# A recurrent-memory transformer layer on one core: the forward output projection in 256-column halves, a float32 memory selection, and row sums on GpSimd

## The chip, the cores and the metric

The kernel runs on one core of a Trainium2 chip. Times are device microseconds of one execution of the whole program. The kernel before was run three times; the median is compared. Profiled executions are read from the hardware profiler's trace: its span runs from the first to the last instruction.

Engine names: PE is TensorE (matmuls; PEld are its weight loads), DVE is VectorE, ACT is ScalarE, POOL is GpSimd, SP is SyncE, which issues most DMAs.

## The reference

One layer and its backward pass are computed: a residual, a recurrent attention branch with memory, and a dense branch with a squared ReLU, then all gradients.

```python
# x (1,2048,512); mem0 (1,8,512); 32 heads of 128; segments of 32 tokens
xn = layernorm(x)
mem = mem0
for s in range(64):
    h = concat([mem, xn[:, 32*s:32*s+32]])        # 8 + 32 rows
    q, k, v = h @ Wq, h @ Wk, h @ Wv              # per head
    p = softmax(mask(q @ k.T * scale))
    o = einsum('bhte,hed->btd', p @ v, Wo)        # sum over 32 heads
    mem = o[:, :8]                                # memory of the next segment
    outs.append(o[:, 8:])
out = x + concat(outs) + mlp(xn)
# then the gradients of x, mem0, Wq, Wk, Wv, Wo and of the dense branch
```

The memory makes the 64 segments a sequential chain: the projections of segment s+1 need rows 0 to 7 of the output projection of segment s.

## The kernel before

**Stages.** The program has five: the dense branch and the layer norm (0 to some 230 us of the span), the forward recurrence (to some 1310 us), a stretch in which weights are turned for the backward pass (to some 1345 us), the backward recurrence (to some 2515 us), and the weight gradients (to the end). Partial results pass between the stages through DRAM tensors whose names begin with S_. Every instruction is unrolled.

**Order.** In the forward and backward stages every operation is given to a planner (`_Plan`, `plan.add`) with a cost for each engine that may run it, the keys that it reads and writes, and a priority. The planner simulates the engines with these costs, chooses an order by the longest remaining path plus a number for each kind of operation (a lift; the lists `_FWD` and `_BWD`, with rules and biases beside them), and writes the instructions out in that order. On the chip each engine and each DMA queue then runs its own list in order; a DMA that waits on SP or POOL holds back everything behind it in that queue. The costs steer the order only.

**The chain of a segment** (`chain(s)`). Rows are packed 32 to a segment and four segments to a block of 128 tokens, 16 blocks in all. In a segment's 32 rows, rows 0 to 7 hold the memory and rows 8 to 31 hold tokens 8 to 31. Tokens 0 to 7 of the four segments of a block, 32 rows too, are computed apart from the recurrence in `l_proj`/`l_qkv` and `l_attn` (the "L" part), one block later. The chain projects q, k and v with matmuls of 32 weight columns, four of them side by side in the array; transposes q and k (line 382); computes scores (L1019, L1027) and a softmax on DVE and ACT (L894 to L900); multiplies by v in 32x32 tiles (`diag`, L533); evicts to `oN`, transposes it on DVE to `OT` (L475); and multiplies by Wo.

**The output projection** (`wo_part`, L910). For each of 8x4 heads it issues four matmuls of 128 columns, one for each quarter `jd` of the 512 output columns; each quarter goes to its own 32 partitions, and PSUM sums over all heads: 128 matmuls and 128 weight loads. The result is a 128x128 tile, partition 32*jd + row. In the chain the memory rows then go on: an eviction to bfloat16 (`mbA`, in the tile PB of the profile; lines 386 or 388), one PE transpose (L382), and a DVE copy of 32 columns to `hA` (L1047; hA is in the tile PA). The next segment's projections read `hA`. The token rows are added to the residual and dense part on DVE (`obA`, L1049; `obL`, L993, in the L part) and leave by DMA in pieces of 128 columns.

**DMA.** Each segment stores q, k, v, p and o; each block loads the residual rows `sbA` and `sbL` (through S_BL), stores `obA` to the output and `obL` to S_OL, and loads and stores others. S_OL is copied to the output at the end of the backward stage. Beside the chain, the forward stage computes two weight gradients of the dense branch (`dw_unit`, L1105, whose inputs `sx` come by DMA), and GpSimd (POOL) copies a few tiles and issues the DMAs of those results.

The backward stage has a like step: its partial sums `R_A` stay float32 and a float32 matmul with a selection matrix (`sel8`, L1384) both sums the partials and picks the eight memory rows.

Of the kernel before, what the change touches and what calls it, by code (L numbers as in the profile page):

```python
# [9 lines left out]
ALU = mybir.AluOpType  # L10
# [6 lines left out]
P = 128  # L17
# [19 lines left out]
)  # L37
_FWD_RULE = (0.298, 0.516, 1.499, 3.394)
_FWD_BIAS = (-0.118, -0.036)
_BWD = (  # L40
# [12 lines left out]
)  # L53
_BWD_RULE = (0.029, 3.877, 0.329, 0.734)
_BWD_BIAS = (0.007, -0.09)

class _PE(dict):
    shape = None


def pe(cost, shape):
    x = _PE(PE=cost)
    x.shape = shape
    return x


# [191 lines left out]
def kernel(  # L258
# [70 lines left out]
    def dt_(shape, dt, name):  # L329
        return dram.tile(shape, dt, name=name)  # L330
# [1274 lines left out]
```

## Time and profile before

| what | us |
|---|---|
| runs of the kernel before | 3068.97, 3072.24, 3077.88 (median 3072.24) |
| the profiled execution, its own time | 3071.63 |
| the span of the profiled execution | 3069.9 |
| PE busy over the span | 2731.8 (89%) |
| mean granted clock of TensorE | 0.966 |
| forward, 240 to 1300 us: PE, DVE, ACT, POOL busy | 920.95, 529.02, 407.40, 27.00 of 1060 |
| backward, 1345 to 2515 us: PE, DVE, ACT, POOL busy | 1002.84, 536.73, 397.74, 91.27 of 1170 |

A row of a group reads: line, engine, operation, tile written <- tiles read, shapes, count; then the busy time and the mean of one in ns; then the idle time of the engine before them and what ended it. "issue" as a releaser is time in which the engine waited for nothing that the profile shows. A row of the timeline begins with its start and its length in us. Rows of the queues give packets, megabytes and share.

### The profile page before, as it was taken

To read this page: it belongs to the slowest core of one execution; us is meant where nothing else is said; L and a number is where in the kernel's file an instruction comes from. 1 tells how busy PE (TensorE), PEld (TensorE's weight loads), DVE (VectorE), ACT (ScalarE), POOL (GpSimd) and SP (SyncE) were. 2 spreads that over 40 slices of the span, in tenths; PEclk is the share of its full clock that TensorE was granted. 3 is DMA by queue.
4 is the path that set the end of the run, shared out by engine and by line. 5 is a ranking of instruction groups with operands and counts; after the bars stand their busy time and mean duration, and the time that the engine had idled before them with its cause. 6 is when DMAs were issued, how large, how long until landed. Compare 5 with 4: busy or idle time off the path is not lost. (4 is left out here: it accounts for less than half of the span.)

```text
span 3069.9 us, 138767 instructions
## 1 busy us (share of the span) xinstructions
PE 2731.8 (89%) x62715; PEld 1505.3 (49%) x62847; DVE 1376.5 (45%) x3386; ACT 945.0 (31%) x1813; POOL 259.5 (8%) x434
## 2 busy tenths in 40 slices
PE   8998888998888888888888888888888889999999
PEld 6664454554545455564444444444444444444444
DVE  5544445455545454574444444444444421232322
ACT  4333333343434344333333333333333310000000
POOL 1110000000000000100000000000000001221111
PEclk9999999999999999999998999999999999999999
DMA  6648656566655555457877777777777789788861
GB/s 206 218 145 227 160 160 164 150 176 156 163 161 154 141 166 148 146 133 198 216 194 194 194 204 211 212 200 204 213 204 205 205 272 335 246 255 282 248 182 45
DMA packets 554919, 590.55 MB, mean 192 GB/s; under 512 B 250197, under 2 KB 355110, under 8 KB 552150
## 3 DMA queue, kind: packets, MB, share of 16 engines
q1 hardware_dynamic: 538758, 527.06, 61.6%
q0 software_dynamic: 15568, 54.61, 5.3%
q8 instruction: 491, 8.04, 1.2%
q14 instruction: 102, 0.84, 0.1%
HBM read 283.32 MB, written 262.68 MB: 178 GB/s over the span
## 5 line engine op out<-in xcount | busy, mean ns | idle before, releaser
L1213 PE MATMUL ps<-WA,dT 128*32 128x512 bf16 x6144 | 419.2, 421 | 16.0 <-issue 12.6
L492 PE MATMUL ps<-WA,PA 128*32 128x512 bf16 x6144 | 378.8, 388 | 13.8 <-issue 7.2
L1552 PE MATMUL ps<-WA,WB 128*128 128x512 bf16 x1536 | 332.3, 379 | 0.6 <-DVE gwo L386 0.6
L492 PEld LDWEIGHTS <-PA 128*32 128x32 bf16 x8192 | 210.3, 98 | 216.9 <-issue 33.5
L1552 PEld LDWEIGHTS <-WB 128*128 128x128 bf16 x1896 | 185.4, 98 | 224.9 <-issue 1.7
L388 ACT CAST dN<-ps 128x512 bf16<-128x512 f32 x316 | 173.1, 588 | 360.0 <-issue 245.9
L1213 PEld LDWEIGHTS <-dT 128*32 128x32 bf16 x6144 | 161.3, 104 | 217.3 <-issue 83.7
L386 DVE CAST gwo<-ps 128x512 bf16<-128x512 f32 x64 | 39.8, 684 | 398.8 <-PE ps L1552 268.7
L475 DVE STREAM_TRANSPOSE dT<-dN 128x256 f32<-128x256 f32 x384 | 156.7, 426 | 93.2 <-ACT dN L388 90.9
L388 ACT CAST gwo<-ps 128x512 bf16<-128x512 f32 x64 | 33.0, 599 | 515.3 <-PE ps L1552 385.4
L910 PE MATMUL ps<-WB,OT 128*32 128x128 bf16 x8192 | 141.6, 226 | 52.2 <-issue 27.3
L910 PEld LDWEIGHTS <-OT 128*32 128x32 bf16 x8192 | 124.5, 100 | 78.9 <-DVE OT L475 43.7
L1326 POOL COPY bVT<-VR 128x1024 bf16<-128x1024 bf16 x64 | 66.6, 1041 | 860.6 <-PE ps L1349 823.8
L492 PE MATMUL ps<-WB,PA 128*32 128x512 bf16 x2048 | 125.5, 384 | 3.6 <-DVE PA L1387 1.2
L388 ACT CAST gON<-ps 128x512 bf16<-128x512 f32 x128 | 75.0, 586 | 173.5 <-PE ps L492 167.1
L386 DVE CAST kN<-ps 128x512 bf16<-128x512 f32 x62 | 42.9, 692 | 182.4 <-PE ps L492 176.9
L533 PEld LDWEIGHTS <-PB 32*32 32x32 bf16 x8192 | 71.2, 88 | 108.4 <-issue 53.8
L1105 PE MATMUL ps<-sx,anT 128*128 128x512 bf16 x352 | 105.3, 382 | 19.0 <-DMA sx<-in_grad_out_dram 13.2
L1213 PE MATMUL ps<-WA,LT 128*32 128x512 bf16 x1536 | 108.7, 388 | 5.3 <-issue 5.0
L492 PE MATMUL ps<-WA,PB 128*32 128x512 bf16 x1536 | 109.1, 384 | 4.4 <-issue 3.5
L386 DVE CAST dN<-ps 128x512 bf16<-128x512 f32 x68 | 46.6, 685 | 144.3 <-PE ps L533 127.7
L1556 PE MATMUL ps<-GOc,WA 128*128 128x512 bf16 x486 | 106.9, 379 | 0.5
(282 smaller groups left out, 4177.5 us busy)
## 6 DMA issues: line engine op xcount, KB each, us to landing
S_GN<-dN SPq DMA_DIRECT2D x192, 256.0 KB
WA<-S_GN SPq DMA_DIRECT2D x160, 256.0 KB
S_K<-kN SPq DMA_DIRECT2D x64, 256.0 KB
S_Q<-qN SPq DMA_DIRECT2D x64, 256.0 KB
S_V<-vN SPq DMA_DIRECT2D x64, 256.0 KB
S_ON<-oN SPq DMA_DIRECT2D x64, 256.0 KB
bkN<-S_K SPq DMA_DIRECT2D x64, 256.0 KB
bqN<-S_Q SPq DMA_DIRECT2D x64, 256.0 KB
```

What stands on the lines that cost most here:

```text
L386: nc.vector.tensor_copy(out, in_)
L388: nc.scalar.copy(out, in_)
L475: self.plan.add({"DVE": 0.42}, lambda e, x=x: nc.vector.transpose(dst[:, x, :, :].rearrange("p i c r -> p (i c r)").bitcast(F32).rearrange ...
L492: nc.tensor.matmul(bk()[32 * j:32 * (j + 1), :], lhsT=win(dc), rhs=Wt(dc, c0), start=(dc == 0), stop=(dc == DC - 1), tile_position=(0, 32 ...
L533: nc.tensor.matmul(self.ps[32 * c:32 * c + m, pairs[r // 2][r % 2], x * P:(x + 1) * P], lhsT=lf(r, i), rhs=rf(r, i), start=(x == 0 and y = ...
L910: nc.tensor.matmul(bk()[32 * jd:32 * (jd + 1), :], lhsT=tq(OTt, i, j), rhs=Wo[:, JQ * hs(i) + j, jd * P:(jd + 1) * P], start=(i == 0 and j ...
L1105: nc.tensor.matmul(bks[x]()[:], lhsT=anT[x][:, c, :], rhs=sx[z][:], start=(c == 0), stop=(c == TC - 1))
L1213: nc.tensor.matmul(bk()[32 * j:32 * (j + 1), :], lhsT=tq(XT, i, j), rhs=wtf(t, JQ * hs(i) + j), start=(first and i == 0), stop=(last and i ...
L1326: A({"POOL": 1.0}, lambda e: nc.gpsimd.tensor_copy(VT[:, :, :, M:KA].rearrange("p i j r -> p (i j) r"), VR[:].rearrange("p i j r -> p (i j ...
L1552: nc.tensor.matmul(bks[n]()[:], lhsT=HNc[:, rc, dc * P:(dc + 1) * P], rhs=half_of(gns[y], hf), start=(y == 0), stop=(y == NRC - 1))
L1556: nc.tensor.matmul(bks[n]()[:], lhsT=gns[y][:, k * P:(k + 1) * P], rhs=GOc[:, rc, :], start=(y == 0), stop=(y == NRC - 1))
```

## The change

1. **Projection by halves.** `wo_part` issues, for each head, two matmuls of 256 columns (h = 0, 1) in place of four of 128. Half h of heads with even j goes to partition group 2h, of odd j to 2h+1, so that each half is left as two partial sums over heads. The tile is 128x256 float32; the eviction goes to a float32 SBUF tile (`RFA` in the chain, `RFL` in the L part).
2. **Memory rows.** The bfloat16 eviction, the transpose and the copy become: the float32 eviction, eight float32 matmuls (`gm`: weights are 32-column pieces of RFA, the moving operand is the 128x16 selection matrix `selF`), which add the two partial sums and pick the eight rows, and the DVE copy to `hA`.
3. **Token rows.** RFA (each segment) and RFL (each block) are stored to a DRAM tensor S_RO; one block later `out_sum` loads the residual rows to `sumB` and, for each half, both partial sums to `sumR`, adds them on GpSimd, and stores 128 rows of the output with one DMA. sbA, sbL, obA, obL, S_BL, S_OL and the copy at the end of the backward stage go. In the last block these DMAs are issued by POOL, else by SP.
4. **L scores** take one matmul of 64 columns for each head in place of two of 32.
5. **Planner.** Costs of evictions and of the DVE transposes are lowered and a latency is added to them; all numbers of `_FWD`, `_BWD` and their rules and biases differ, so that the order differs in both stages. A softmax tile shares a buffer with another, and one padded probability tile moves to PB.

```diff
-_FWD_RULE = (0.298, 0.516, 1.499, 3.394)
-_FWD_BIAS = (-0.118, -0.036)
+_FWD_RULE = (0.306, 4.312, 1.123, 6.993)
+_FWD_BIAS = (-0.197, -0.188)
...
-    EV_F = {"DVE": 0.70, "ACT": 0.59}
-    EV_B = {"DVE": 0.44, "ACT": 0.59}
+    EV_F = {"DVE": 0.62, "ACT": 0.49}
+    EV_B = {"DVE": 0.36, "ACT": 0.49}
+    EVLAT = 0.09
...
+        RFA, RFL = tl("RFA", [P, HB], F32), tl("RFL", [P, HB], F32)
+        selF = tl("selF", [P, 2 * M], F32)
...
+        sumR, sumB = tl("sumR", [P, 2, HB], F32), tl("sumB", [P, D])
...
-            bk = sg.bank(kind, [P, P], F32, "ps_R" + nm)
+            bk = sg.bank(kind, [P, HB], F32, "ps_R" + nm)
             for q in range(4):
                 def mm(e, q=q):
                     for i in (2 * q, 2 * q + 1):
                         for j in range(JQ):
-                            for jd in range(DC):
+                            for h in range(2):
+                                t = 2 * h + j % 2
                                 nc.tensor.matmul(
-                                    bk()[32 * jd:32 * (jd + 1), :], lhsT=tq(OTt, i, j),
-                                    rhs=Wo[:, JQ * hs(i) + j, jd * P:(jd + 1) * P],
-                                    start=(i == 0 and j == 0), stop=(i == NI - 1 and j == JQ - 1),
-                                    tile_position=(0, 32 * jd),
+                                    bk()[32 * t:32 * (t + 1), :], lhsT=tq(OTt, i, j),
+                                    rhs=Wo[:, JQ * hs(i) + j, h * HB:(h + 1) * HB],
+                                    start=(i == 0 and j < 2), stop=(i == NI - 1 and j > 1),
+                                    tile_position=(0, 32 * t),
                                 )
-                A(pe(0.5, "w"), mm, [(ok, q // 2), "WB"], [bk.key], prio)
-            return bk
+                A(pe(0.435, "w"), mm, [(ok, q // 2), "WB"], [bk.key], prio, 0.3)
+            A({"ACT": 0.34, "DVE": 0.36}, lambda e: ev({"DVE": "v", "ACT": "s"}[e], out[:], bk()[:]), [bk.key], [okey], prio, EVLAT)
+
+        def out_sum(b, tail):
+            q = "POOL" if tail else "SP"
+            c = T_DMA + tail
+            sg.dma(lambda: sumB[:], lambda: S_B[b * P:(b + 1) * P, :], [], ["sumB"], cost=c, eng=q)
+            for h in range(2):
+                sg.dma(lambda h=h: sumR[:], lambda h=h: S_RO[b, h].rearrange("y p d -> p y d"),
+                       [("RO", b, v) for v in range(SPB)] + [("RO", b, "L")], ["sumR"], cost=c, eng=q)
+                A({"POOL": 0.9}, lambda e: nc.gpsimd.tensor_tensor(
+                    out=sumR[:, 0, :], in0=sumR[:, 0, :], in1=sumR[:, 1, :], op=ALU.add), [], ["sumR"])
+                A({"POOL": 0.9}, lambda e, h=h: nc.gpsimd.tensor_tensor(
+                    out=sumB[:, h * HB:(h + 1) * HB], in0=sumR[:, 0, :], in1=sumB[:, h * HB:(h + 1) * HB], op=ALU.add),
+                  ["sumR"], ["sumB"])
+            sg.dma(lambda: out0flat[b * P:(b + 1) * P, :], lambda: sumB[:], ["sumB"], [], cost=c, eng=q)
...
-            A(pe(0.95, "w"), sc, [("qLT%d" % p, 0), ("qLT%d" % p, 1), ("KTL", p, 0), ("KTL", p, 1)]
+            A(pe(0.55, "w"), sc, [("qLT%d" % p, 0), ("qLT%d" % p, 1), ("KTL", p, 0), ("KTL", p, 1)]
...
-                A({"ACT": 0.27, "DVE": 0.27}, lambda e: ev({"DVE": "v", "ACT": "s"}[e], mbA[:], bR()[:]), [bR.key], ["mbA", ("lock", bR.key)], 0)
-                bm = sg.bank("c", [P, DC, RA], BF16, "ps_mem")
-                A(pe(0.08, "f"), lambda e: transpose_to(bm()[:].rearrange("p c r -> p (c r)"), mbA[:]), ["mbA"], [bm.key], 0)
+                bm = sg.bank("c", [P, 2, 2, M], F32, "ps_mem")
+
+                def gm(e):
+                    for a in range(2):
+                        for g in range(JQ):
+                            nc.tensor.matmul(bm()[32 * g:32 * (g + 1), a].rearrange("p h m -> p (h m)"),
+                                             lhsT=RFA[:, a * P + 32 * g:a * P + 32 * (g + 1)], rhs=selF[:],
+                                             start=(a == 0), stop=(a == 1), tile_position=(0, 32 * g), skip_group_check=True)
+                A(pe(0.5, "w"), gm, ["RFA"], [bm.key], 0)
...
-            A({"DVE": 0.27}, lambda e: V.tensor_tensor(out=obA[p][:, v, :], in0=bR()[:], in1=sbA[p][:, v, :], op=ALU.add),
-              [bR.key] + [("sbA", p, jd) for jd in range(DC)], [("obA", p, v), ("lock", bR.key)], 1)
+            sg.dma(lambda: S_RO[b].rearrange("h y (v r) d -> v (h y) r d", r=RA)[v],
+                   lambda: RFA[:], ["RFA"], [("RO", b, v)])
...
-        sg.dma(lambda: seg_rows(out0flat, SEG, 0, M), lambda: seg_rows(S_OL, M, 0, M), [("gm", 0, SPB - 2)], [])
```

More of the change, by code (lines that the diff above doesn't have):

```diff
@@ L337 @@
     S_B = dt_([S, D], BF16, "S_B")
-    S_OL = dt_([TC * RL, D], BF16, "S_OL")
-    S_BL = dt_([TC * RL, D], BF16, "S_BL")
+    S_RO = dt_([TC, 2, 2, P, HB], F32, "S_RO")
     S_GXNB = dt_([S, D], F32, "S_GXNB")
@@ L854 @@
         for v in range(SPB):
[L855 to L856 removed]
+            t_ = (fw.tile([P, NI, RL], BF16, name="PLp%d" % v)[:] if v else
+                  pb_rest[:, HW // 2:HW // 2 + NI * RL].rearrange("p (i k) -> p i k", i=NI))
+            nc.vector.memset(t_, 0.0)
             PLp.append(t_)
@@ L875 @@
         PLL, PTLL = tl("PLL", [P, NI, 2 * RL]), tl("PTLL", [P, NI, 2, RL])
-        sbA = [tl("sbA%d" % x, [P, SPB, P]) for x in range(2)]
-        obA = [tl("obA%d" % x, [P, SPB, P]) for x in range(2)]
-        mbA = pb_rest[:, 512:512 + P]
-        sbL, obL = tl("sbL", [P, P]), tl("obL", [P, P])
+        RFA, RFL = tl("RFA", [P, HB], F32), tl("RFL", [P, HB], F32)
+        selF = tl("selF", [P, 2 * M], F32)
+        nc.gpsimd.memset(selF[:], 0.0)
+        for g in range(JQ):
+            h = g // 2
+            nc.gpsimd.affine_select(
+                selF[:, M * h:M * (h + 1)], selF[:, M * h:M * (h + 1)], pattern=[[-1, M]], compare_op=ALU.not_equal,
+                fill=1.0, base=-32 * g, channel_multiplier=1
+            )
+        sumR, sumB = tl("sumR", [P, 2, HB], F32), tl("sumB", [P, D])
         hN = tl("hN", [P, D])
@@ L988, in l_attn @@
             sg.sq_T(oLN, "lN0", qLT[p], "qLT%d" % p, 1)
-            for jd in range(DC):
-                sg.dma(lambda jd=jd: q_(sbL, jd), lambda jd=jd: S_BL[b * RL:(b + 1) * RL, jd * P:(jd + 1) * P],
-                       [("S_BL", b)], [("sbL", jd)])
-            bR = wo_part("f", "L", qLT[p], "qLT%d" % p, 1)
-            A({"DVE": 0.27}, lambda e: V.tensor_tensor(out=obL[:], in0=bR()[:], in1=sbL[:], op=ALU.add),
-              [bR.key] + [("sbL", jd) for jd in range(DC)], ["obL"])
-            for jd in range(DC):
-                sg.dma(lambda jd=jd: S_OL[b * RL:(b + 1) * RL, jd * P:(jd + 1) * P], lambda jd=jd: q_(obL, jd), ["obL"], [],
-                       cost=T_DMA + (b == TC - 1), eng="POOL" if b == TC - 1 else "SP")
-        def blk_rows(ap, b, r0, r1, jd):
-            x = ap[b * P:(b + 1) * P, jd * P:(jd + 1) * P]
-            return x.rearrange("(v r) d -> r v d", r=SEG)[r0:r1]
+            wo_part("f", "L", qLT[p], "qLT%d" % p, 1, RFL, "RFL")
+            tail = b == TC - 1
+            sg.dma(lambda: S_RO[b].rearrange("h y (v r) d -> (h y) v r d", r=RA)[:, :, 0:M],
+                   lambda: RFL[:], ["RFL"] + [("RO", b, v) for v in range(SPB)], [("RO", b, "L")],
+                   cost=T_DMA + tail, eng="POOL" if tail else "SP")
+            out_sum(b, tail)
         def chain(s):
@@ L1060, in chain @@
                        [(nm, s)], [(nm + "M", b, v)])
-        def blk_in(b):
-            p = b % 2
-            for jd in range(DC):
-                sg.dma(lambda jd=jd: q_(sbA[p], jd), lambda jd=jd: blk_rows(S_B, b, 0, SEG, jd), [], [("sbA", p, jd)])
         def blk_out(b):
@@ L1069, in blk_out @@
             tail = b == TC - 1
-            for jd in range(DC):
-                sg.dma(lambda jd=jd: blk_rows(out0flat, b, M, SEG, jd), lambda jd=jd: obA[p][32 * jd + M:32 * (jd + 1)],
-                       [("obA", p, v) for v in range(SPB)], [], cost=T_DMA + tail, eng="POOL" if tail else "SP")
             bk = sg.bank("f", [P, D], BF16, "ps_hN")
```

49 lines of the change are left out of this document (23 added, 26 removed), and 44 rows, old and new, of tables (_BWD, _FWD).

## The prediction

> **What bounds the kernel now.** I read the page first (busy shares, instruction queue), then the sums by stretch, then the forward waits of PE, then single segments in the timeline.
>
> ```profile
> PE 2731.8 (89%) x62715; PEld 1505.3 (49%) x62847; DVE 1376.5 (45%) x3386; ACT 945.0 (31%) x1813; POOL 259.5 (8%) x434
> q8 instruction: 491, 8.04, 1.2%
> L910 PE MATMUL ps<-WB,OT 128*32 128x128 bf16 x8192 | 141.6, 226 | 52.2 <-issue 27.3
> ```
>
> The sums by stretch, in us: PE, PEld, DVE, ACT, POOL busy, then the granted clock, the DMA share and GB/s:
>
> ```profile
> 240.00:1300.00 1060.00, 920.95 (x27915) 536.89 (x28009) 529.02 (x1314) 407.40 (x743) 27.00 (x52) 0.98 0.58 161
> ```
>
> PE looks like the bound at 89%, but in the forward stretch it is 87% busy with matmul latencies in that figure, and the stage is a chain. The 63 copies L1047 that hand the memory on start between 251.3 and 1282.6 us: 16.63 us a segment, while the quickest segments follow each other in 14.7 to 15.1. Adding one undisturbed segment's steps in the timeline (projections 3.6, evictions and transposes, scores, softmax, diag, projection by Wo, memory) also gives about 15. So latency counts in full, and about 1.6 us a segment (some 100 in all) are disturbances. The waits of PE, 240 to 1300 us, name them:
>
> ```profile
> PE ps L910 <- issue: 33.5, 38, 2.4
> PE ps L533 <- DMA VM<-S_VM: 13.4, 9, 4.3
> PE ps L1105 <- DMA sx<-in_grad_out_dram: 13.2, 9, 2.6
> ...
> PE ps L492 <- issue: 10.7, 17, 2.2
> ```
>
> The largest is "issue" inside the Wo projection. Two segments of the timeline, a clean one and a held one:
>
> ```profile
> 910.70 1.97 PE L910 MATMUL ps<-WB,OT 128*32 128x128 bf16 x128
> ...
> 781.53 0.91 PE L910 MATMUL ps<-WB,OT 128*32 128x128 bf16 x52 [0.89 <-DVE OT L475]
> 784.00 1.97 PE L910 MATMUL ps<-WB,OT 128*32 128x128 bf16 x76 [1.56 <-issue]
> ```
>
> 128 matmuls take 1.97 when nothing interrupts; here PE stops for 1.56 with its operands ready. Over all 64 segments the span from first start to last end of this group has mean 2.67 and least 1.97 by the trace's records: 0.70 x 64 = **45 us** lost on the chain. I read it as instruction supply. Queue 8 moved 8.04 MB, which is 64.0 bytes for each of the page's 125,562 PE and PEld rows, in 491 packets of 256 instructions. A Wo projection is 256 instructions in 1.8 us: a packet for every one. In the packet records the hold above ends 1.41 us after a packet landed (781.62 to 782.59), the hold of 2.24 before 718.96 ends 1.39 after one (716.45 to 717.57); most others in L910 show the same 1.4. With 1.1 median in flight, a packet needs some 2.5 us, more than the 1.8 in which the projection eats one.
>
> **The change, part by part.**
>
> *Memory path: +36 us.* Before, from the start of the mbA eviction to the end of L1047 the median is 0.79. After: the float32 eviction of 256 columns (R_A row: ACT 0.373, DVE 0.425), the selection, and a copy like L1387 (0.192). The backward stage shows the last two:
>
> ```profile
> 2010.78 0.65 ACT L388 COPY R_A<-ps 128x256 f32<-128x256 f32 x2 [2.54 <-PE ps L1213]
> 2011.20 0.97 PEld L1384 LDWEIGHTS ps<-sel,R_A 128*128 128x128 f32 x8 [0.36 <-ACT R_A L388]
> 2011.20 1.06 PE L1384 MATMUL ps<-sel,R_A 128*128 128x8 f32 x8 [0.19 <-ACT R_A L388]
> 2012.30 0.19 DVE L1387 CAST PA<-ps 128x32 bf16<-128x32 f32 x1 [0.82 <-PE ps L1384]
> ```
>
> Four float32 matmuls appear as eight pairs of load and matmul, (1.06-0.26)/7 = 0.114 us apart. The eight new ones are then 16 pairs, with 32 weight columns in place of 128. Float32 loads cost by column (192 ns at 128 columns in L1384, 88 at 8 in L1391), so the pitch I take is a quarter, 0.0285: 15 x 0.0285 + 0.26 = 0.69. Bounds: the pitch of L910's pairs, 0.014 (0.47 in all), and the unscaled 0.114 (1.97). Sum: 0.373+0.69+0.192 and 0.11 for three handovers = 1.36, which is +0.57; 63 of them +36 (bounds +22 and +117). Nothing hides it: the next projections wait, and only L or dw matmuls can fill PE.
>
> *Instruction supply: -43.* The projection falls to 64 matmuls and 64 loads. Per page of 256 there is then always other work, at least a diag (128 instructions), the eviction and DVE transposes between (some 1.9 us), and the projection (1.9): over 4 us for a packet that needs 2.5. I let an eighth of the 45 remain, -40, and -3 of the 17.6 us of other "issue" waits (L492, L533), because the forward stage has fewer pages: -10,240 (Wo) -1,024 (L scores) -126 (transposes) +2,016 (selection) = -9,374 instructions, 37 of its 219 packets (17%). Bounds: -8 (17% of 45, if only the number counts) and -48.
>
> *Clean projection: -4.* In L492 sixteen groups of four 512-column matmuls take 3.64 (64 matmuls), so a group is (3.64-0.38)/15 = 0.217, half as wide 0.109; 15 x 0.109 + 0.27 = 1.90 against 1.97, 64 times.
>
> *L part: -8.* Its L910 rows are 36.5 us busy where 16 x 1.97 would be 31.5, and 7.7 idle at issue: I take half of 13, as it is beside the chain, and 16 x 0.07 = 1. L scores (L975, 11.2 us) halve at best; off the chain, -1.
>
> *DVE and DMA removed: -3.* The obA adds (0.28 x 64) lie behind the chain's eviction on a DVE busy half the time: 0; they would cost up to 18 only on a full DVE. DVE waited 5.5 us in kN evictions whose last releaser was the sbL load, which goes: -3. SP issues 9 transfers a block for this work, not 17, at some 0.4 each. Bytes rise: 1,408 KB a block (stores 640, partial loads 512, sumB and output 256) for 352, 17 MB in all; the DMA engines are 58% busy in this stretch, so 0 while that cover lasts.
>
> *Token sums: +7.* A GpSimd float32 add of 256 columns has no row; POOL copies 128x256 bf16 in 0.40, four times that (twice the bytes, two inputs) is 1.6, and I take 0.8. 3.2 us a block on an engine 27 us busy of 1060 is hidden, except where it blocks others. SP's load of the second half waits for POOL's adds, and behind it in SP's queue stand sx, VM and the q/k/v stores; PE waits for the first two. Two waits of some 0.5 us a block, a fifth of them felt: +3 (bounds 0 and +26, 0.8 x 2 x 16). At the end POOL runs four DMA round trips (0.55 issue, 2.0 landing, as S_OL's) and four adds, 13 us, ahead of the backward stage's first bVT copy (1314.8); PE turns weights until the first projection at 1332.7, so +2 (bounds 0 and +6). DVE: +2 for a softmax multiply (0.49) now and then held by POOL; bounds 0 and 16 x 3.2 = +51. The Trainium skill (SBUF — State Buffer, "Who interferes with whom") speaks against the change here: DVE operations with two SBUF inputs and GpSimd operations that read SBUF exclude each other for a whole instruction. No run here shows it yet; without that rule the +2 would be 0.
>
> *Order: 0.* All lifts differ in both stages. What they can move are waits: forward VM and sx (26.6 us), backward some 167 us of PE idle in 1170. I take 0, with -25 and +20 as ends. The final S_OL copy (one SP issue of 0.58) is lost in this.
>
> Sum: 36-43-4-8-3+7 = **-15**, against the profiled execution's 3071.6 (span 3069.9 and 1.7 around it; 0.6 under the median): 3057.
>
> **Rivals.**
>
> *The stalls stay* (slower). If the hold is not the supply of the projection itself, or if it passes to the next dense run (diag, selection) on the chain, only 17% of the 45 goes: 3057 + 48 - 8 = 3097. It decides as soon as less than 33 of the expected 48 us (43, and 5 in the L part) come back. For: L533 holds too, with 128 instructions in half a microsecond. Against: the 1.4 us after landings, and 38 of PE's 60 issue holds are in L910. The Trainium skill (Runtime: NRT & Kernel Launch, "Instruction fetch mechanics") has blocks of 256 instructions too, but says that their fetch is hidden by the sequencer's own pace; by that this rival would be the forecast. The 8.04 MB agree with the block, the holds after landings do not agree with the hiding.
>
> *The selection keeps its pitch* of 0.114: +81, 3138. Against: the loads that scale with columns.
>
> *The order gains*: VM and sx waits go, 3032. For: the quick segments of 14.7 show room. *The order loses*, 20 us: 3077. For: more transfers and waits in a like plan. *SP stands behind POOL*: +26, 3083. Against: SP already waits 96.6 us for DVE's kN from 230 to 1310 us, mostly unfelt.
>
> **How the numbers follow.** Forecast 0.38, stalls stay 0.20, order gains 0.17, order loses 0.10, SP behind POOL 0.08, pitch 0.07. 0.3% is 9 us, about what a measurement of this kernel tells from no change: 3063 to 3081 is the same. The forecast's own range, 3040 to 3075, lies two thirds below 3063: 0.25, with the order's gain 0.17 and 0.03 of the rest makes 0.45 faster. Same: 0.11 of the forecast and 0.08 of the order's loss and SP, 0.19. Slower 0.36. The range 3024 to 3104 holds all but the pitch, the far end of stalls and the far end of order.
>
> **What would show it.** L910 with 64 matmuls a segment, 1.9 us each, few rows split by "issue"; f32 PE rows of some 0.7 us after each; copy to copy near 16.4 us on average and none under 15.2; forward queue-8 packets down by 37; sumR and sumB with POOL adds of 0.8 us. It is wrong if "issue" in forward stays over 35 us, if the selection takes over 1 us, or if the backward stretch moves by more than 20 us.

## The result and the profile after

In the first session the changed kernel took 3042.44 us (median of four, 3025.66 to 3051.52), the kernel before 3074.99 (four, 3068.97 to 3077.88): ratio 0.989, 95% interval 0.9844 to 0.9937. In two later sessions the changed kernel was run beside the kernel before again: 0.9931 (0.9898 to 0.9963) and 0.9929 (0.9901 to 0.9957). So it is faster by about 0.7 to 1.1%, 20 to 33 us. The forecast was 3057 in a range of 3024 to 3104. The kernel before stood at 3075, 3051, 3048 and 3054 in the four sessions (the record names chip 15 for the second and the fourth, chip 5 for the third, none for the first), so below only kernels of one session are compared in us, and ratios otherwise. Ratios and intervals are the record's, over all runs of both kernels; they can differ by up to 0.15% from the quotient of two medians.

From the page of the kernel after, the busy shares, the instruction queue and the row of the projection:

```profile
PE 2726.4 (89%) x58160; PEld 1500.4 (49%) x58160; DVE 1326.6 (44%) x3255; ACT 968.0 (32%) x1881; POOL 303.7 (10%) x500
...
q8 instruction: 454, 7.44, 1.1%
...
L920 PE MATMUL ps<-WB,OT 128*32 128x256 bf16 x4096 | 136.1, 289 | 30.2 <-ACT oN L388 16.7
```

PE is as busy as before (2726 us against 2732), with 4,555 fewer matmuls: a busy share that does not move says nothing here. The packets of queue 8 went from 491 to 454, the 37 fewer that were counted. The projection's row no longer ends its idle time on "issue". The same stage by the sums by stretch (PE, PEld, DVE, ACT, POOL, clock, DMA share, GB/s) of the kernel after:

```profile
240.00:1250.00 1010.00, 907.21 (x23572) 532.87 (x23575) 464.42 (x1136) 470.15 (x876) 70.83 (x117) 0.98 0.66 185
```

The forward stage now ends at 1252 us, not 1306, in 4,343 fewer PE rows (27,915 to 23,572), at the same granted clock. What PE waited for there, kernel after, 240 to 1250 us (total, times, longest):

```profile
PE ps L534 <- DVE PB L1048: 19.0, 24, 2.2
...
PE ps L534 <- DMA VM<-S_VM: 14.3, 11, 3.0
PE ps L493 <- DVE qLT L386: 13.3, 1, 13.3
...
PE ps L1118 <- DMA sx<-S_XN: 3.7, 4, 1.3
PE ps L920 <- issue: 3.6, 4, 1.4
...
PE ps L1118 <- DMA sx<-in_grad_out_dram: 2.0, 2, 1.1
PE ps L534 <- issue: 1.5, 2, 0.8
```

"Issue" fell from 33.5 to 3.6 us in the projection and from 10.7 to 0.8 in the projections of q, k and v (L492 before, L493 after); the waits for `sx` fell from 15.5 to 5.7, that for `VM` stayed. A new wait of 13.3 us stands there once, at the start of the stage.

A clean segment in the timeline of the kernel after:

```profile
902.42 1.93 PE L920 MATMUL ps<-WB,OT 128*32 128x256 bf16 x64
...
904.40 0.37 ACT L388 COPY RFA<-ps 128x256 f32<-128x256 f32 x1 [1.22 <-PE ps L920]
...
904.83 0.40 PEld L1063 LDWEIGHTS ps<-selF,RFA 128*32 128x32 f32 x16
905.04 0.28 PE L1063 MATMUL ps<-selF,RFA 128*32 128x16 f32 x16
...
905.42 0.19 DVE L1067 CAST PA<-ps 128x32 bf16<-128x32 f32 x1 [2.73 <-PE ps L1063]
```

The projection is a row of 64 matmuls in 1.93 us, as foreseen (1.90), and the memory path takes 1.21 from the start of the eviction (904.40) to the end of the copy (905.61).

Fifty-two of the 64 projections take 1.93 or 1.94; twelve take 2.8 to 3.6. The sums by stretch of the kernel after, over a projection that takes 3.59 and over the clean one (the clock stands before the DMA share):

```profile
1132.40:1136.10 3.70, 3.64 (x72) 2.97 (x76) 0.66 (x3) 0.01 (x1) 0.00 (x0) 0.54 0.63 161
...
902.40:904.40 2.00, 2.00 (x75) 1.83 (x74) 0.29 (x1) 0.58 (x1) 0.00 (x0) 1.00 0.54 186
```

The granted clock is 0.54 there, and the matmuls follow each other at an even, slower pace: groups of four 0.19 apart where the clean ones are 0.11 apart. Eight of the twelve are of this kind. Only four show one gap with PE at a stop (0.86 to 1.64 us from one matmul's start to the next). Before, 33 of 64 showed such a gap, and five the slower pace.

Cut at the copies to the memory rows (forward: L1047 before, L1067 after) and at the backward stage's copies to `gT` (L1387, L1398), the spans of the two profiled executions divide so:

| part (us) | before | after | difference |
|---|---|---|---|
| start to the first memory copy | 251.3 | 265.2 | +13.9 |
| 62 forward segments, copy to copy | 1031.3 (16.63 each) | 965.8 (15.58) | -65.5 |
| last memory copy to first `gT` copy | 82.8 | 78.5 | -4.3 |
| 62 backward segments | 1107.9 (17.87) | 1142.1 (18.42) | +34.2 |
| last `gT` copy to the end | 596.6 | 598.0 | +1.4 |
| span | 3069.9 | 3049.6 | -20.3 |

The 62 forward segments gained more than four times the 15 us that the forecast had in all, and 48 us were lost at two places that the forecast had put at nothing. The profiled execution of the kernel after, 3051.52, is the slowest of its four runs; the other executions profiled below show how far the backward pitch varies.

### The profile page after: what moved, and what is told of

It is laid out like the page before. It is cut to its first block, busy times and chain, and to the rows that moved or that the text cites. A ratio compares the mean times of both kernels' runs of the same rounds, so it can differ in the third digit from the quotient of the medians.

```text
span 3049.6 us, 129655 instructions
## 1 busy us (share of the span) xinstructions
PE 2726.4 (89%) x58160; PEld 1500.4 (49%) x58160; DVE 1326.6 (44%) x3255; ACT 968.0 (32%) x1881; POOL 303.7 (10%) x500
## 5 line engine op out<-in xcount | busy, mean ns | idle before, releaser
L493 PE MATMUL ps<-WA,PA 128*32 128x512 bf16 x6144 | 364.2, 382 | 8.7 <-DVE PA L1067 7.7
L493 PEld LDWEIGHTS <-PA 128*32 128x32 bf16 x8192 | 203.3, 97 | 211.8 <-DVE PA L1067 24.7
L388 ACT CAST dN<-ps 128x512 bf16<-128x512 f32 x287 | 159.5, 588 | 394.3 <-PE ps L534 183.4
L920 PE MATMUL ps<-WB,OT 128*32 128x256 bf16 x4096 | 136.1, 289 | 30.2 <-ACT oN L388 16.7
L386 DVE COPY qT<-ps 128x512 bf16<-128x512 bf16 x128 | 54.3, 424 | 248.5 <-PE ps L382 243.2
L386 DVE CAST dN<-ps 128x512 bf16<-128x512 f32 x97 | 66.8, 689 | 177.4 <-PE ps L534 177.3
L920 PEld LDWEIGHTS <-OT 128*32 128x32 bf16 x4096 | 110.7, 102 | 53.6 <-DVE OT L476 44.0
L493 PE MATMUL ps<-WB,PA 128*32 128x512 bf16 x2048 | 127.5, 391 | 1.9 <-DVE PA L1398 0.6
L1118 PE MATMUL ps<-sx,anT 128*128 128x512 bf16 x448 | 113.9, 381 | 6.0 <-DMA sx<-S_XN 3.7
L388 ACT CAST qN<-ps 128x512 bf16<-128x512 f32 x128 | 74.9, 585 | 131.4 <-PE ps L493 130.8
L493 PE MATMUL ps<-WA,PB 128*32 128x512 bf16 x1536 | 99.4, 385 | 13.7 <-DVE qLT L386 13.3
## 6 DMA issues: line engine op xcount, KB each, us to landing
S_GN<-dN SPq DMA_DIRECT2D x192, 256.0 KB
WA<-S_GN SPq DMA_DIRECT2D x160, 256.0 KB
S_K<-kN SPq DMA_DIRECT2D x64, 256.0 KB
S_Q<-qN SPq DMA_DIRECT2D x64, 256.0 KB
S_V<-vN SPq DMA_DIRECT2D x64, 256.0 KB
S_ON<-oN SPq DMA_DIRECT2D x64, 256.0 KB
bqN<-S_Q SPq DMA_DIRECT2D x64, 256.0 KB
bkN<-S_K SPq DMA_DIRECT2D x64, 256.0 KB
```

What stands on the lines that cost most here:

```text
L386: nc.vector.tensor_copy(out, in_)
L388: nc.scalar.copy(out, in_)
L493: nc.tensor.matmul(bk()[32 * j:32 * (j + 1), :], lhsT=win(dc), rhs=Wt(dc, c0), start=(dc == 0), stop=(dc == DC - 1), tile_position=(0, 32 ...
L920: nc.tensor.matmul(bk()[32 * t:32 * (t + 1), :], lhsT=tq(OTt, i, j), rhs=Wo[:, JQ * hs(i) + j, h * HB:(h + 1) * HB], start=(i == 0 and j < ...
L1118: nc.tensor.matmul(bks[x]()[:], lhsT=anT[x][:, c, :], rhs=sx[z][:], start=(c == 0), stop=(c == TC - 1))
```

## The experiments

Theory after the first look: the forward gain is instruction supply, larger than forecast; the start loses some 10 us to a clearing that waits for a transfer; the backward stage loses 20 to 30 to its new order. Rivals: that the forward gain is the new order; that the backward loss is a scatter or a matter of the transfers left over from forward.

### The kernel after again: a_copy, a_copy2

No edit.

> The changed kernel again, to see which stage its scatter of 26 us (3025.66 to 3051.52) lies in. If it lies in the backward stage, the 62 steps from the first to the last float32 memory copy of the backward chain, 18.42 us each in the first profile, come out between 18.0 and 18.5, and the forward steps at 15.6 again. If it lies in the forward stage, those 15.58 move by 0.2 or more.

3026.71 us (3023.5 to 3035.48), before there 3051.51: 0.9931.

> The kernel after as it is, as the measure for the other three on this chip: 0.987 to 0.995 of before, forward pitch 15.4 to 15.6.

3034.28 us (3023.41 to 3047.44), before there 3053.83: 0.9929. Forward pitch 15.47 and 15.60, first memory copy at 264.5 and 264.2, backward pitch 18.10 and 18.41. The forward gain and the late start are the kernel's; the backward pitch differs from execution to execution by 0.3, but stays above the 17.87 of before.

### The projection split again: a_wo128

Each 256-column matmul is issued as two of 128 columns; the plan, the eviction, the selection and the row sums are those of after.

```diff
-for h in range(2):
+for c, h in ((0, 0), (0, 1), (1, 0), (1, 1)):
     t = 2 * h + j % 2
-    matmul(bk()[32*t:32*(t+1), :], lhsT=tq(OTt, i, j), rhs=Wo[..., h*HB:(h+1)*HB], ...)
+    matmul(bk()[32*t:32*(t+1), c*P:(c+1)*P], lhsT=tq(OTt, i, j), rhs=Wo[..., h*HB+c*P:h*HB+(c+1)*P], ...)
```

> The changed kernel with each 256-column matmul of the Wo projection issued as two of 128 columns into the same place: the same sums, the same order by the planner, 128 matmuls and 128 loads a segment again. Theory (instruction supply): the projection's mean span goes from 2.18 back to 2.6 or 2.7 us, forward holds at issue from 6 back to 40 us or more, total +30 to +45 us. Rival (the forward gain is the new order or the shorter chain): span 2.2, total within 8 us of the changed kernel.

3106.10 us (3102.69 to 3114.78), 79 over a_copy in the same session, well over the 30 to 45 that were expected, and 1.0194 of before (1.0168 to 1.022). Its PE waits by "issue", 240 to 1300 us:

```profile
PE ps L920 <- issue: 26.5, 33, 2.0
...
PE ps L534 <- issue: 12.3, 9, 2.2
...
PE ps L1063 <- issue: 7.8, 7, 1.7
...
PE ps L493 <- issue: 6.6, 10, 1.8
```

These 53 us are the 53.6 of the kernel before over again (35.0, 10.7 and 7.9 by the same view, 240 to 1310), where after has 6. The packet records tell what ends them: of the 55 "issue" waits over 0.25 us between 240 and 1310 us, 54 end 1.1 to 1.7 us after a packet of the instruction queue has landed, and of the 56 of the kernel before, 54. These packets land 4.8 us apart on average, so at a time picked at random that would hold in one case of eight. The forward pitch goes from 15.47 to 16.67, 62 x 1.20 = 75 of the 79 us. By the mean steps of a segment the 1.20 are: the projection itself +0.51, from its end to the memory copy +0.31, q and k projections, evictions and transposes +0.24, the eviction to `oN` +0.08, the wait before the first projection +0.05. The clock has a share in it: at half speed it stood for 47 us of these 62 segments against 27 in a_copy, and by a fit over the segments a us at half speed lengthens a segment by 0.36 to 0.48, which is 7 to 10 of the 75. So as much as the whole forward gain of the change, and more, hangs on the width of these matmuls. What the rest of the change did in this stage about cancels: with the old width, a_wo128 has nearly the pitch of before (16.67 against 16.63); from its projection's end to the memory copy it is 0.32 longer than before (20 us), from the memory copy to the softmax 0.29 shorter (18 us). Whether the new order made the second shorter, or the L scores or the transfers that went, was not separated: the forward order was not run alone. And a hold of PE costs more than its own row: matmuls of the L part that stand ahead of the selection or of the next q matmuls hold those back too. Between the eviction to RFA and the end of the selection a_wo128 has 18 us of "issue" in all, 10 of them ahead of the selection, a_copy 1.

### Half of it split: a_wo96

```diff
+for c, h in (((0, 0), (0, 1), (1, 0), (1, 1)) if q < 2 else ((0, 0), (0, 1))):
```

> The kernel after, with the first half of each Wo projection split (the first two of four parts, 32 matmuls of 256 columns as 64 of 128), the second half left whole: 64 more instructions per segment, 192 in a projection where after has 128 and a_wo128 256. If the stalls grow evenly with the instructions: half of a_wo128's 79, so 35 to 45 us over the kernel after. If a threshold decides (a projection of 192 instructions in 1.9 us leaves a packet of 256 its 2.5 us): 0 to 20 us.

3055.52 us (3050.03 to 3067.95), 21 over a_copy2 (0.8% by the two ratios, 25 us), pitch 15.89 against 15.60 (18 us). "Issue" in 240 to 1300 us is 16.5 in all (9.2 in the projection), against 2.6 in a_copy2 and 53 with all of it split. Half the added instructions bring 21 to 25 of 79 us: it grows faster than their number. That lies between the two theories, just above the 20 that the threshold had been given and well under 35; a sharp threshold is not shown.

### As many instructions at an idle place: a_slack

```diff
-sg.proj("c", "v", win, ..., ("vN", vN), 0)
+sg.proj("c", "v", win, ..., ("vN", vN), 0, more=lambda: [
+    matmul(ps[32*(k%4):32*(k%4+1), <bank of the scores>, 320:336], lhsT=ident[:, ...32 columns], rhs=mk[:, 0:16],
+           start=False, stop=True, ...) for k in range(64)])
```

> The kernel after, with 64 tiny matmuls (32x128 times 128x16, each with its load) added behind the v projection of every chain segment, into columns that nobody reads: 128 more instructions per segment, as many as the split projection of a_wo128 adds, but at a place where PE stands about 2 us before diag can start, waiting for the softmax. They take about 64 x 14 ns = 0.9 us there. Theory A of the prediction (what counts is a dense run that eats a page faster than the next one comes): 0 to 20 us over the kernel after, forward pitch 15.5 to 15.8, the split cost 79. Rival B (only the number of instructions per segment counts, wherever they stand): the greater part of a_wo128's 79 us, 50 or more, forward pitch 16.3 or more, with waits called issue back in the stage.

3092.02 us (3089.76 to 3097.35), 58 over a_copy2: by the total, the rival. But the trace shows another cause. The row of the softmax's first operation, in 240 to 1300 us, first in a_copy2, then in a_slack, where L1047 is the line of the added matmuls:

```profile
L903 DVE TENSOR_REDUCE mxA<-ps 128x8 f32<-128x320 f32 x64 | 31.4, 491 | 27.7 <-PE ps L1041 27.7
```

```profile
L905 DVE TENSOR_REDUCE mxA<-ps 128x8 f32<-128x320 f32 x64 | 31.5, 492 | 75.2 <-PE ps L1047 67.8 <-PE ps L1043 7.4
```

The reduction waits for the added matmuls, which write to spare columns of the tile that it reads; so they did not lie in the idle place but ahead of the softmax. By the steps of a segment, scores to reduction is 0.77 longer and reduction to `P` 0.26: 1.03 in all, where the pitch is 0.93 longer (16.53 against 15.60, 62 x 0.93 = 58 us). These two steps are the whole loss. The waits called issue in a_slack:

```profile
PE ps L998 <- issue: 5.0, 4, 2.0
PE ps L493 <- issue: 4.7, 5, 1.9
...
PE ps L1047 <- issue: 2.8, 2, 1.8
PE ps L922 <- issue: 2.1, 5, 0.7
```

With 0.3 more in diag that is 15 us, against 53 in a_wo128, though the instruction queue carries nearly as many packets (486 and 494; after 454). The same number of instructions away from the projection brings a quarter of the holds, which speaks for the dense run and against the number alone. The total itself can't be used, since the edit put a wait of its own on the chain.

### The order numbers of the backward stage: a_bwd0, b_bwd1

a_bwd0 is the kernel after with the kernel before's `_BWD` numbers, rule, biases and costs in the backward stage (the costs of the diff stand in that stage only); b_bwd1 is the kernel before with those of after. No operation is added or taken away.

```diff
-_BWD_RULE = (0.035, 3.044, 0.368, 0.96)
+_BWD_RULE = (0.029, 3.877, 0.329, 0.734)
...
+    EV_F, EV_B = {"DVE": 0.70, "ACT": 0.59}, {"DVE": 0.44, "ACT": 0.59}
+    EVLAT, SQC, SQLAT = 0.0, 0.42, 0.0
```

> The changed kernel with the numbers of the kernel before for the planner in the backward stage (lifts, rule, bias, costs); the forward stage is untouched. Theory (the backward order alone lost the time): backward steps return from 18.42 to 17.87 us, 62 x 0.55 = 34 us, so about 3010 to 3020 us. Rival (the backward stage lost it to something that the forward stage leaves behind, or it is scatter): steps stay near 18.4 and the time near 3042.

3004.42 us (2995.83 to 3017.7), 22 under a_copy in the same session, 0.986 of before (0.9827 to 0.9893). Backward pitch 17.88.

> The kernel before, with the changed kernel's order numbers and cost figures for the backward stage only; forward is the kernel before, and no operation is added or removed. If the backward order that came with the change is a loss of its own (the kernel after with before's numbers was 22 us quicker than its sibling on one chip), this comes out 14 to 34 us over before, and the gT copies follow each other in 18.1 to 18.5 us where before shows 17.87. Rival: those numbers only lose beside the changed forward stage and the partial sums around them (the backward stage of after has the same operations, but starts with other transfers under way): then 0 +- 8, with a pitch of 17.8 to 18.0.

3078.25 us (3059.11 to 3083.24) where before stood at 3048.43: 1.0092 (1.0064 to 1.0121), 28 us slower by the ratio (30 by the medians). Backward pitch 18.10. The loss is the order's own, with or without the changed forward stage. The sums by stretch of the backward segments, before and then b_bwd1:

```profile
1355.00:2475.00 1120.00, 961.02 (x28892) 516.95 (x28888) 519.04 (x1234) 383.63 (x738) 90.27 (x140) 0.94 0.77 202
```

```profile
1340.00:2475.00 1135.00, 968.68 (x28920) 519.66 (x28921) 543.30 (x1295) 347.91 (x678) 91.09 (x140) 0.93 0.76 200
```

The changed costs and numbers moved some 60 evictions from ACT to DVE (738 to 678, 1234 to 1295). In PE's waits by "issue" the last projection of the backward segment is held longer, `diag` less. First before, then b_bwd1:

```profile
PE ps L533 <- issue: 63.3, 52, 3.7
...
PE ps L1213 <- issue: 17.6, 24, 2.2
```

```profile
PE ps L535 <- issue: 57.9, 51, 3.4
PE ps L1217 <- issue: 25.4, 28, 2.5
```

So these waits do not grow as a whole: over the 62 backward segments they are 87 us before and 85 in b_bwd1, 91 in a_bwd0 and 78 in the slower a_copy. In b_bwd1 a segment is 0.23 us longer: the mean end of the transposes to `dT` is 0.13 late and the projection after them adds 0.09; the selection and copy behind it take the same. In a_copy against a_bwd0 (0.22 longer) these transposes end 0.14 earlier and the projection adds 0.29. Only the stretch from the last transpose to the end of that projection is longer in both pairs. The segments give 62 x 0.23 = 14 us of the 28 and 62 x 0.22 = 14 of the 22; the profiled executions of a_copy and a_bwd0, 19 us apart, have the rest ahead of the backward segments (5 us), and for b_bwd1 there is no profile of before from its session. The clock is the smaller part: it stood at half for 143 us of the backward segments before and 157 in b_bwd1 (147 in a_bwd0, 167 in a_copy), and at the 0.3 us that one us of it costs here, by a fit over the segments, that is 4 to 6 of the 14. Segments with the full clock throughout have a mean of 16.94 before and 17.38 in b_bwd1, 17.11 in a_bwd0 and 17.34 in a_copy. That the order costs the time is shown; which of the moved operations does it was not tried and stays open.

### The clearing at the start: a_pl

One padded tile, PLp0, stands in the buffer PB in after, and PB also stages a transfer to the output just before the stage. The timeline of the kernel after:

```profile
247.48 0.17 DVE L858 MEMSET PB<- 128x128 uint32 x1 [16.97 <-DMA out_dram<-PB]
...
248.00 2.32 PE L493 MATMUL ps<-WA,PB 128*32 128x512 bf16 x20 [13.32 <-DVE qLT L386]
```

DVE stands for 17 us at a clearing until that transfer is out, and the first evictions and PE behind it. a_pl gives PLp0 its own tile and puts PLp3 there instead, cleared by an operation of the second segment; the two small results that wait in PB for their transfer take another place in it.

```diff
-t_ = fw.tile(...) if v else pb_rest[...]
-nc.vector.memset(t_, 0.0)
+t_ = fw.tile(...) if v + 1 < SPB else pb_rest[...]
+if v + 1 < SPB:
+    nc.vector.memset(t_, 0.0)
...
+if b == 0 and v == 1:
+    A({"DVE": 0.1}, lambda e: V.memset(PLp[SPB - 1], 0.0), ...)
```

> The changed kernel, with the padded probability tile of the first segment in a tile of its own again; that of the fourth segment takes the place in PB and is cleared later, and the two small results that wait in PB for their DMA move out of the way. Theory (the 13.3 us for which PE stands still at 235 us is DVE, held by clearing a part of PB that a DMA still reads): the hold goes, the first memory copy starts near 251 us and not at 265, total -13 us against the changed kernel. Rival (the start waits for something else, as the Wo load): the first copy stays at 262 or later, and the total within 5 us.

The wait is gone and the first memory copy comes at 254.3 us, 10 earlier than in a_copy; the total is 3023.94 (3014.72 to 3039.2), 3 under a_copy, with intervals that overlap widely (0.9919, 0.989 to 0.9948, beside 0.9931, 0.9898 to 0.9963). By the two profiles 8.6 of the 10 us are still there at the first `gT` copy (1293.4 against 1302.0) and 3.7 at the last one, where the backward pitch of a_pl happened to be higher (18.18 against 18.10), with the same backward order. So the late start costs 10 us at its place and most of it reached the backward stage here; that it reaches the total is not shown.

### The selection twice: a_gm2

```diff
-for a in range(2):
+for a in (0, 1, 0, 1):
```

> The kernel after, with the selection matmuls of the memory path issued twice into the same place, the second over the first: 16 more pairs on the chain per segment, nothing else altered. In the profile of after 16 pairs take 0.29 to 0.4 us. Theory that the forward stage is one chain on which latency counts in full (the prediction's ground for its +36): 63 x 0.25 to 0.45, so 16 to 28 us over the kernel after, with the copies to the memory rows some 0.25 to 0.45 us further apart (15.75 to 16.0 where the sibling showed 15.47). Rival: the chain has slack there (other waits end later), and 5 us or less come out. 2,016 more instructions would by the instruction supply alone add under 10.

3040.46 us (3023.39 to 3051.73), 0.9965 of before (0.9938 to 0.9993) where the kernel after had 0.993 in other sessions: 0.35%, about 11 us, with intervals that overlap. The timeline of a_gm2:

```profile
902.52 0.44 PE L1063 MATMUL ps<-selF,RFA 128*32 128x16 f32 x32
```

Sixteen more pairs take 0.16 us (0.44 against 0.28), 10 ns a pair, so the dose was smaller than the expectation made it. The median from the eviction's start to the copy's end goes from 1.17 to 1.31, 63 x 0.14 = 9 us. The forward pitch is 15.67, under the 15.75 that was expected and 0.07 to 0.2 over the kernel after's in three profiles (15.47 to 15.60), which is 4 to 12 us. So the dose comes out in size, as it would if latency on this path counts one to one; but it is no larger than the scatter of the kernel after, and the rival of 5 us or less is not excluded.

### Without the GpSimd additions: a_noadd, a_noadd2

```diff
-A({"POOL": 0.9}, lambda e: nc.gpsimd.tensor_tensor(out=sumR[:, 0, :], ...), [], ["sumR"])
-A({"POOL": 0.9}, lambda e, h=h: nc.gpsimd.tensor_tensor(out=sumB[:, h*HB:(h+1)*HB], ...), ["sumR"], ["sumB"])
+A({"POOL": 0.9}, lambda e: None, [], ["sumR"])
+A({"POOL": 0.9}, lambda e, h=h: None, ["sumR"], ["sumB"])
```

> The kernel after, without the four GpSimd additions per block of partial sums: the transfers stay, and the output lacks the sums over the other heads. Prices what the prediction called token sums (+7, of it +3 for SP behind POOL, +2 for DVE multiplies held by POOL, +2 at the end of the forward stage): by it 2 to 7 us less than the kernel after. Rival 1: POOL holds DVE for whole additions (11 us of additions per block, bounded in the prediction at +51): 20 to 50 us less, and the softmax multiplies in forward visibly shorter. Rival 2: all hidden, within 3 us.

3018.57 us (3012.53 to 3026.23), 0.9897 of before (0.9855 to 0.9938), with no kernel after in that session. The expectation's 11 us of additions per block is a slip: the rows below give 2.8. The ratio leaves it open, so it was run beside the kernel after:

> The kernel after without the four GpSimd additions per block once more (the output lacks the sums over the other heads), now beside the kernel after on the same chip. The first time it stood at 0.9897 of before where the kernel after on another chip stood at 0.9931, but its forward pitch was no shorter (15.58 against 15.47). If the additions cost what the prediction put on them: 2 to 7 us less than a_copy2; if the first ratio was right: 8 to 12 less; if hidden: within 3.

3035.13 us against 3034.28 of a_copy2: no difference, with about 11 us of scatter on either side by the intervals (0.9908 to 0.9959, beside 0.9901 to 0.9957). Forward pitch 15.61 against 15.60. The rows of the additions in the kernel after:

```profile
L936 POOL TENSOR_TENSOR sumR<-sumR 128x256 f32<-128x256 f32 x32 | 23.2, 724 | 566.7 <-DMA sumR<-S_RO 566.7
L938 POOL TENSOR_TENSOR sumB<-sumR,sumB 128x256 bf16<-128x256 f32 x32 | 21.4, 670 | 2.5
```

These are 45 us of additions, on an engine that is idle nine tenths of the stage. The pair speaks for hidden and excludes the 20 to 50 us of rival 1; it can't tell nothing from the 2 to 7 us of the prediction.

### Both losses undone: a_best

The edits of a_bwd0 and a_pl together.

> The kernel after with two parts put back: the backward order numbers and costs of the kernel before, and the heap of PL rows whose clearing stood behind a transfer at the start in a tile of its own, so that no clearing waits for the transfer out. If the two effects add (22 and 3 to 10 us on the first chip): 0.978 to 0.985 of before, 46 to 68 us under it, first copy to the memory rows near 254 us, gT copies 17.8 to 17.95 us apart. Rival: the start gives back what it gains, as in the run that had it alone, and this is no quicker than the order alone (0.986).

2992.96 us (2981.44 to 3000.19) where before stood at 3048.43: 0.9808 (0.9764 to 0.9852), 55 us faster and the quickest of all kernels here. First memory copy at 256.0, backward pitch 17.86. Beside a_bwd0 (0.986, 0.9827 to 0.9893, another chip) the placement would add some 16 us by the two ratios, but the intervals overlap; by the two profiles the first memory copy comes 9 us earlier and the first `gT` copy 2.8. What the placement adds to the order in the total is open.

## Why the prediction was right, and where it was not

The total came out inside the range and in the direction: -15 was summed, the profiled execution moved by -20, the medians by -33 in the first session and some -21 in the two later ones. But the sum was right by two errors of one size that cancel, and that is luck. The forward segments and what follows each recurrence came out 53 us better than the sum had them (-68 against -15), the start and the backward segments 48 worse than the nothing that stood for them.

**What bounds the kernel.** Right as far as it was tested. The forward stage is a chain: the split projection came out with more than its own holds. That latency of the memory path counts one to one is what the doubled selection suggests (9 us added, about 11 measured), inside its scatter.

**Instruction supply, -43.** Right in kind, and two of its parts mis-sized in opposite directions. In the projection, 45 us were put down to supply, of which an eighth was to remain. By the trace of before, 36 of them are gaps, 7 the slower pace at half clock (the granted clock over such a projection, 1163.1 to 1166.8, is 0.54 there too), and one is other matmuls between. Of the 36, 4.7 remain in the kernel after: seven eighths went, as forecast. But the forecast took the clock for supply: the granted clock of the held stretches was not read. Its share rose from 7 to 11 us, so that the mean span fell from 2.67 to 2.18, 31 us in 64, and not 44. The other step that failed is "-3 of the 17.6 us of other issue waits": nearly all of them went (10.7 to 0.8 and 6.9 to 1.5), and with them the time by which held matmuls of the L part and of the selection itself made the memory path and the next q and k late, 0.31 and 0.24 us a segment in the split kernel, 34 us. The prediction counted each hold where it stood and not what queued behind it. In all, the split kernel loses 79 us, where the sum had 55 for the same (43, 4 for the clean projection, 8 for the L part).

**The rule that speaks against it.** The Trainium skill (Runtime: NRT & Kernel Launch, "Instruction fetch mechanics") says that the fetch of blocks of 256 instructions is mostly hidden, and by it the rival "the stalls stay" (3097) would have been the forecast. Here 128 added PE instructions per projection cost 79 us with 53 us of waits at "issue", nearly all of which end at one distance behind a landed packet, so the fetch was not hidden. The rival fell: of the forward "issue" waits 6 us are left.

**Memory path, +36.** Mis-sized, and on the low side of its own bounds. The path's median went from 0.79 to 1.17 us: +0.38 x 63 = 24, near the lower bound of 22. The pitch of the selection pairs was put at 0.0285 by scaling the loads with their columns; the doubled selection gives 0.010, lower even than the 0.014 that was taken for the least. The rival "the selection keeps its pitch" fell with it. The mean of this path hardly moved (1.14 to 1.16), because before had holds of 0.35 on average in it (mean 1.14 against median 0.79): pricing the new path against the clean old one was right only as long as those holds were booked elsewhere, and they were not.

**L part, -8, and DVE and DMA removed, -3.** Not tested alone. The 7.7 us of "issue" ahead of the L projection's row are gone; its busy time went from 36.5 only to 34.9 us, where the forecast halved the excess over 31.5.

**Token sums, +7.** Probably too high: no difference by the pair of runs (3035.13 against 3034.28), which could not have told 7 us from nothing. The additions take 0.72 and 0.67 us. That 0.8 was near is luck, since the working gave 1.6 and was halved without a reason. `sx` stands behind those loads in SP's queue, yet PE's waits for it are 5.7, 8.1 and 13.0 us in the three profiles of the kernel after, 15.5 in that of before, and 13.8 and 7.4 without the additions: none grew beyond before, and they do not go with the additions. The rival "SP behind POOL" fell. The Trainium skill (SBUF — State Buffer, "Who interferes with whom") has DVE and GpSimd exclude each other at a shared port; in the three profiles of the kernel after only 1 of 192 softmax multiplies of the chain and 2 of 192 subtractions ran beside an addition, at their usual 0.49 us, and the multiplies have a mean of 492 ns with and without the additions. No run here shows a price of it.

**Order: 0.** Wrong as a term for the backward stage, open for the forward one. Forward, 75 us by the width of the matmuls less 24 for the memory path make 51 of the 65 gained; the other 14 (21 by the profile of a_copy) belong to the order, the L part, the transfers that went or scatter, and no run divides them. Backward the order cost 22 us one way round and 28 the other, slightly over the +20 that was the worst end. That an order can lose was the rival "order loses" (3077, chance 0.10), but it was argued by more transfers and waits, and b_bwd1 loses without one transfer more. What the traces show is 60 moved evictions and a later end of the last projection; what inside the order does it stays open.

Two of the prediction's signs came out otherwise: copy to copy was to be 16.4 on average and never under 15.2, and is 15.58 with clean segments from 14.8; and the backward stretch moved by the 20 us and more that were to mean an error. The rival "order gains" (3032) lies nearer to the first session's median than the forecast does (10 us against 15), but its ground, the `VM` and `sx` waits, gave 3 to 9 us in all (28.9 to between 20.0 and 25.6), and the width of the matmuls the most.

**What was not priced.** "One padded probability tile moves to PB" stood in the change and got no line in the sum. It put a clearing behind a transfer at the start: 17 us of DVE, 13 of PE, first memory copy 10 to 14 us later.

## What to carry to other kernels

Where a trace shows PE waiting for nothing in a run of many small instructions, count 256-instruction pages against the time in which they are eaten; halving the instructions of that run may be worth more than the waits in its own row, since everything queued behind a held instruction on the same engine is late too. By the same sign the next place to look in this kernel is `diag` in the backward stage: it waits 63 us at "issue" in before and 52 in a_copy, and of the backward "issue" waits over 0.25 us in before 73 of 76 end 1.1 to 1.7 us after a packet has landed. No run tried it. Regenerated order numbers are a part of a change and are priced by running them alone, in both directions, for the stage whose work did not change: here the backward ones took back about half of the gain (0.9931 with them, 0.986 without). A buffer that is reused at the border of two stages is priced by asking what its first writer waits for.

## What the hardware showed that was not expected

- Float32 matmuls of 32 weight columns and 16 moving columns, four side by side, follow each other at 10 ns a pair (sixteen more pairs in 0.16 us), where the 128-column ones of the backward stage's selection stand 114 ns apart.
- Instructions added to a dense run on PE cost more than evenly: 64 more in a projection (32 matmuls and their loads) 21 to 25 us, 128 more 79. The holds end 1.1 to 1.7 us after a packet of the instruction queue has landed, in 54 of 55 cases of a_wo128's forward stage.
- An order with the same operations is worth 0.7 to 0.9% of the time of this kernel, and its backward pitch varies by 0.4 us between the profiled executions with after's numbers (18.05 to 18.42) but not with those of before (17.86 to 17.88 in three).
- The granted clock drops to half for stretches of 3 to 14 us in forward and backward alike (51 us of the forward segments before, 27 to 34 in three profiles of the kernel after; 143 to 195 of the backward ones); by fits over the segments a us of it costs the chain 0.2 to 0.5 us. In the timeline it looks like a hold, and only the even pace and the clock column tell the two apart.
- The level of one and the same kernel differs by 0.9% between sessions (3048 to 3075), as much as the whole change is worth.
